# Attention and a spectral filter interleaved on one core: a constant table loaded later, softmax normalization with due times, and a newly searched order

## The chip, the core and the metric

The kernel runs on one core of one Trainium2 chip. The metric is device time in microseconds of one execution. A core has five engines with a queue of instructions each: TensorE (PE) for matrix products, VectorE (DVE), ScalarE (ACT), GpSimd (POOL) and SyncE (SP), which here only issues DMA transfers. An instruction waits on semaphores that other engines or transfers raise, and every queue is worked off strictly in order.

## The reference

Two independent computations are put side by side in the output, 2048 rows of 448 + 448 columns.

```python
# A: attention, S = 2048, D = 448, 16 heads of 28
q, k, v = split(A_x @ A_wqkv)
p = softmax(q @ k^T * 28 ** -0.5)
a = (p @ v) @ A_wo
# B: a filter in the frequency domain, S = 2048, D = 448
X = rfft2(B_x) * (B_w_r + 1j * B_w_i)
b = irfft2(X, s=(2048, 448))
out = concatenate([a, b], axis=-1)
```

## The kernel before, in words

**Attention.** The heads are taken in 4 groups of 4 and the queries in 4 chunks of 512, which gives 16 blocks. In a block, keys come in 16 chunks of 128. A unit is one head, one key chunk and 512 queries: its scores fill one of the 7 working PSUM banks (L1083). For most units ACT computes the exponential, two or three banks in one instruction (L1109), into a ring of 14 SBUF buffers. For a few key chunks in each block (`DN`, L304, usually 3 of 16) DVE does it instead: one instruction turns scores into integers whose bits read as a bf16 power of two (L1119), three more make shifted copies of a pair of units (L1127), and four products with scaled copies of V average the error away. DVE's units have 8 buffers. The products of both kinds accumulate in the eighth bank, `ACC` (L1178), where a column of ones in V gives the softmax sums; a block's products are all made before the next block's begin.

**End of a block.** `finish` (L1202) copies `ACC` to a buffer `oaug` (DVE, L1281), queues a small PE job `n1` that gathers the sums, takes their reciprocal on DVE (L1246), queues a PE job `n2` that spreads them over the partitions (L1255), and multiplies on DVE (L1275). Both jobs are queued with due time -2, ahead of everything else; there are 2 buffers `oaug`. When the last group is done, products with `wo` give the output rows, which are copied and stored.

**Filter.** The transforms along the rows are products with constant tables. Since the transform is symmetric, row n of `B_x` is first added to and subtracted from row 1024 - n (`fold_all`, L653, on POOL). For this, two SyncE transfers (L1409) write rows in reverse order to a DRAM buffer `xrev`: first rows 1 to 255 and then 256 to 511, of two planes each. From there L1413 reads 127 rows and L1414 reads 128 rows of each plane into the tile R1a, and L1416 the rest. Folding writes R1b. Then come products with the 1 MB table FR (`load_f`, L594), a product with T1, the multiplication with the filter W on POOL, and the same back with table T2. W is reversed in DRAM too (`rev_w`, L609).

**How the order is made.** The program that builds the kernel simulates the engines with estimated costs and writes each queue as it goes. `defer` (L149) puts DVE and POOL work in a list with a due time, and `flush` (L186) commits an entry when its inputs are ready by the estimate. `later` (L183) holds a DMA back until its input is ready by the estimate. `dma` estimates a landing as the transfers queued so far, at `kb`/280 us each, plus 2 us plus a `lag`. PE jobs, such as projections or transforms, have due times counted in units that ACT has been given (`st["ai"]`); `JIT` shifts the due times of single jobs, and `PH` places the phases of the filter. [...] Constants set the rest: `FMAX` is the most units of one fill, `TH1` the backlog of ACT from which a single unit may go, `DLEAD` how many units DVE's share may run ahead, and `AL_C` the slack of L1127. A filler product keeps PE active where it would be idle.

Transfers wait for all earlier transfers on their semaphore that were issued when the waiting instruction was written: the first fold with a reversed row therefore waits for both L1413 and L1414 of a plane.

The lines around the moved transfer, in the order in which SyncE gets them:

```python
            for hf in range(2):
                P.dma("sp", ... xrev ..., "d_rv%d" % hf, writes=[("xrev", hf)], kb=2500)
                # held until xrev is ready: L1413, L1414, then L1416 with after=late_loads
        for i in range(2):
            P.dma("sp", ... xE ..., "d_xe", writes=[("xE", i)], kb=2)
        P.dma("sp", ... alt ..., "d_t", writes=["alt"], kb=130)
        load_f(0, 0)
```

## Time and profile before

| | |
|---|---|
| median of 4 runs | 424.44 us (423.23 to 426.2) |
| the profiled execution | 423.46 us, of it 421.7 us span |
| ACT exponentials L1109 | 366 instructions, 384.1 us busy, 828 units |
| of these by shape | 250 of two banks, 106 of three, 10 of one |
| DVE L1119 and L1127 | 196 and 294 instructions, 132.8 and 109.8 us |
| POOL | 190 instructions, 153.3 us |
| first and last exponential | starts at 11.86 us, ends at 413.84 us |
| mean TensorE clock granted | 0.988 |

The profile is one execution. Its busy time is the union of an engine's instructions. The slices cut the span into 40 equal parts of 10.5 us, and a digit is the busy share in tenths. In the list of waits a row reads: engine and line that waited, what released it, total, times, longest, in microseconds. In the order of time a row reads: start, duration, engine, line, operation, tiles written and read, count; in brackets stands how long the engine was idle before and what released it.

### The profile page before, as it was taken

How to read it: one execution, taken by the hardware profiler on the slowest of the kernel's cores; microseconds unless marked ns; L12 is line 12 of the kernel's file. 1: busy time of each engine (PE TensorE's matmuls, PEld its weight loads, DVE VectorE, ACT ScalarE, POOL GpSimd, SP SyncE). 2: the span in 40 equal slices, each digit the busy share in tenths (PEclk: the TensorE clock that was granted, in tenths of full speed). 3: DMA queues.
4: the chain of work that ended last, by engine and by line, in shares of the span. 5: the costliest groups of instructions: out<-in, count | busy, mean ns of one | idle time of the engine just before them, and what ended most of it. 6: DMA issues, size and time to landing. Idle time of an engine off the chain costs nothing.

```text
span 421.7 us, 15264 instructions
## 1 busy us (share of the span) xinstructions
PE 388.1 (92%) x6610; PEld 140.1 (33%) x6611; DVE 341.8 (81%) x717; ACT 388.7 (92%) x374; POOL 153.3 (36%) x190
## 2 busy tenths in 40 slices
PE   8999648999999999899989999999999999989995
PEld 4443212323433333233332333322334333333332
DVE  4789549969697998899869897887898889879972
ACT  2899739999999999999999999999999999999994
POOL 6422054574702554665653455308335100000000
PEclk9999959999999999999999999999999999999999
DMA  9814245200011003400000000000000011101111
GB/s 192 211 49 146 86 143 126 51 4 2 4 38 31 2 3 118 96 3 2 3 2 2 4 2 2 4 2 2 2 3 3 23 35 46 56 24 56 36 45 46
DMA packets 25079, 17.96 MB, mean 43 GB/s; under 512 B 14642, under 2 KB 24372, under 8 KB 24628
## 3 DMA queue, kind: packets, MB, share of 16 engines
q1 hardware_dynamic: 23620, 16.49, 14.0%
q8 instruction: 52, 0.85, 0.8%
q10 hardware_dynamic: 1392, 0.50, 0.5%
q14 instruction: 15, 0.12, 0.1%
HBM read 11.73 MB, written 5.39 MB: 41 GB/s over the span
## 4 chain that ended last, share of the span: by engine, by line
PE 44%; ACT 18%; DVE 13%; SPq 10%; POOL 6%; issue 5%; DMA 2%; ACTq 0%; DVEq 0%; POOLq 0%
ACT ET L1109 17%; PE PS L527 16%; PE PS L1083 14%; PE PS L1178 13%; DVE TT L1127 5%; DVE TT L1119 4%; POOL R1b L664 3%; SPq L1419 2%; DMA R1a<-xrev 2%; SPq L1409 2%; POOL ptmp L664 2%; SPq L1414 2%; SPq L455 2%; POOL R L651 1%; PE PS L1646 1%
## 5 line engine op out<-in xcount | busy, mean ns | idle before, releaser
L1109 ACT ACTIVATE ET<-PS 128x1024 bf16<-128x1024 f32 (+2 forms) x366 | 384.1, 1161 | 19.5 <-PE PS L1083 18.0
L1083 PE MATMUL PS<-qT,kT 28*128 28x512 bf16 x1024 | 141.9, 386 | 21.4 <-DVE TT L1119 9.9
L1119 DVE TENSOR_SCALAR TT<-PS 128x512 int16<-128x512 f32 x196 | 132.8, 685 | 22.9 <-PE PS L1083 21.3
L1127 DVE TENSOR_SCALAR TT<-TT 128x1024 int16<-128x1024 int16 x294 | 109.8, 420 | 17.8 <-POOL R1b L664 12.4
L1178 PE MATMUL PS<-ET,Vaug 128*32 128x512 bf16 x828 | 81.8, 389 | 2.5 <-ACT ET L1109 1.0
L1083 PEld LDWEIGHTS PS<-qT,kT 28*128 28x128 bf16 x1024 | 35.5, 91 | 137.2 <-ACT ET L1109 81.5
L651 POOL TENSOR_TENSOR ptmp<-R1a,R1b 128x450 f32<-128x450 bf16 x32 | 31.4, 995 | 37.9 <-DVE TT L1127 21.4
L1178 PE MATMUL PS<-TT,Vs 128*32 128x512 bf16 x588 | 40.8, 384 | 0.0
L582 POOL TENSOR_SCALAR Vs<-Vaug 128x128 bf16<-128x128 bf16 x42 | 22.2, 530 | 45.3 <-DVE TT L1127 40.8
L527 PE MATMUL PS<-T,R 112*32 112x450 bf16 (+2 forms) x512 | 35.1, 357 | 0.3 <-DVE TT L1119 0.2
L1178 PEld LDWEIGHTS PS<-ET,Vaug 128*32 128x32 bf16 x828 | 21.1, 93 | 42.0 <-issue 31.0
L651 POOL TENSOR_TENSOR R<-R1b 113x512 bf16<-113x512 f32 (+3 forms) x16 | 20.1, 1277 | 27.5 <-DVE TT L1127 17.2
L664 POOL TENSOR_TENSOR ptmp<-R1a 128x448 f32<-128x448 bf16 x16 | 16.4, 1034 | 23.4 <-DMA R1a<-xrev 12.6
L651 POOL TENSOR_TENSOR R1a<-ptmp 128x225 bf16<-128x225 f32 x32 | 18.0, 582 | 18.9 <-DVE TT L1127 16.6
L664 POOL TENSOR_TENSOR R1b<-ptmp 128x448 bf16<-128x448 f32 (+1 forms) x17 | 19.0, 1127 | 6.7 <-DVE TT L1127 6.3
L1178 PEld LDWEIGHTS PS<-TT,Vs 128*32 128x32 bf16 x588 | 15.8, 98 | 14.2 <-DVE TT L1127 0.5
L527 PE MATMUL PS<-FR,R1b 128*32 128x512 bf16 (+1 forms) x256 | 19.7, 382 | 0.6 <-POOL R1b L664 0.5
L651 POOL TENSOR_TENSOR ptmp<-ptmp 128x450 f32<-128x450 f32 x16 | 15.6, 983 | 12.1 <-DVE TT L1127 12.1
L527 PE MATMUL PS<-wv,xAT 128*32 128x112 bf16 x1024 | 19.8, 214 | 0.1
L527 PE MATMUL PS<-FR,R1a 128*32 128x512 bf16 (+2 forms) x256 | 19.7, 383 | 0.1
L1178 PE MATMUL PS<-TT,Vaug 128*32 128x512 bf16 x196 | 19.5, 387 | 0.1
L527 PE MATMUL PS<-xAT,wq 128*32 128x512 bf16 x240 | 18.9, 383 | 0.2 <-DVE TT L1119 0.2
(92 smaller groups left out, 309.4 us busy)
## 6 DMA issues: line engine op xcount, KB each, us to landing
out_dram<-wst SPq DMA_DIRECT2D x30, 112.0 KB, 1.7
FR<-cst_tab SPq DMA_DIRECT2D x3, 1024.0 KB, 7.5
R1a<-in_B_x_dram SPq DMA_DIRECT2D x2, 448.0 KB, 4.5
R1b<-wrev SPq DMA_DIRECT2D x14, 56.2 KB, 2.4
wst<-in_A_wqkv_dram SPq DMA_DIRECT2D x2, 252.0 KB, 3.1
T<-cst_t SPq DMA_DIRECT2D x1, 450.0 KB, 8.2
R1b<-in_B_w_r_dram SPq DMA_DIRECT2D x8, 56.2 KB, 2.2
R1b<-in_B_w_i_dram SPq DMA_DIRECT2D x8, 56.2 KB, 2.1
```

The lines of the kernel that those rows point to most:

```text
L455: P.dma("sp", lambda e: e.dma_start_transpose(xAT[:, 0:3, 512 * n:512 * n + 512], src[:, 0:384]), "d_x%d" % n, writes=[("xAT", n, 0)], kb=700)
L527: ins = e.matmul(out[c:c1], lhsT[:, c:c1], rhs, start=start, stop=stop, tile_position=(0, c))
L582: P.defer("pool", lambda e, ki=ki, kc=kc, c=c: e.tensor_scalar(Vs[:, g % 2, ki, c - 1, :], Vaug[:, g % 2, kc, :], WS[c], None, ALU.mult), ...
L651: P.defer(eng, lambda e: e.tensor_tensor(out, a, b, op), reads=reads, writes=writes, busy=c, allow=allow, port=True, after=after)
L664: P.defer("pool", lambda e: e.tensor_tensor(out, a, b, o), reads=reads, writes=writes, busy=cost, allow=al, port=True, after=after)
L1083: ins = e.matmul(bank(bk), kT[32 * j:32 * j + DH, g % 2, 128 * kc:128 * (kc + 1)], qT[32 * j:32 * j + DH, b % QSL, :], start=True, stop=Tr ...
L1109: P.op("act", lambda e: e.activation(dst, src, ACT.Exp, scale=ESC), reads=[("B", i) for i in o], writes=[("E", p + k) for k in range(n)], ...
L1119: P.defer("dve", lambda e, bk=bk, slot=slot: e.tensor_scalar(TT[:, 0, slot, :], bank(bk), BIAS, 0.0, ALU.add, ALU.max), reads=[("B", bk)], ...
L1127: P.defer("dve", lambda e, c=c, slot=slot: e.tensor_scalar(TT[:, c, slot - 1:slot + 1, :], TT[:, 0, slot - 1:slot + 1, :], SHF * c, None, ...
L1178: ins = e.matmul(ACC[32 * j:32 * j + 32, :], lh, rhs, start=first, stop=last, tile_position=(0, 32 * j))
L1409: P.dma("sp", lambda e, n0=n0, n1=n1: e.dma_start(xrev[:, n0:n1, :], B_x[0].rearrange("(a p) d -> a p d", a=2)[:, 1024 - n0:1024 - n1:-1, :]),
L1414: P.later("sp", lambda e, a=a: e.dma_start(xB[:, a, 1, :], xrev[a - 2, 128:256]), "d_xb%d" % a, [("xrev", 0)], [("xB", a, 1)], 112, lag=1.0)
```

## The change

- `load_f(0, 0)`, the load of the first FR table, moves from its place ahead of the held row transfers into `late_loads`, which runs after the last of them; the other loads in `late_loads` were there already.
- The estimate of the reversal rises from `kb` 2500 to 2650, and the held row transfers are all given a lag of `XLAG` = 3.0 (before: none or 1.0).
- `n1` and `n2` are due 8 and 10 or 18 units later, except in the last group, with 4 buffers instead of 2. (`rb` and `zr`, which this path doesn't use, are not allocated. A form that normalizes two blocks at once is added but off: `PAIR` is `False`.)
- In block 11 DVE takes 3 key chunks instead of 4.
- Output rows of the filter may be copied by ACT once all exponentials have been issued. `YT`, which would move the last such jobs behind the attention, is 0.
- `DLEAD`, `FMAX`, `TH1`, `AL_C` and four entries of `JIT` are new.

```diff
-DN = (3, 3, 3, 3, 3, 3, 3, 3, 3, 3, 2, 4, 3, 3, 4, 3)
+DN = (3, 3, 3, 3, 3, 3, 3, 3, 3, 3, 2, 3, 3, 3, 4, 3)
...
-DBL, NDF, DLEAD = 2.5917, 1, 16
+DBL, NDF, DLEAD = 2.5917, 1, 8
...
-FMAX, FMIN, TH1, RMAX, KEEP, KMIN = 3, 2, 0.4784, 1, 2, 3
+FMAX, FMIN, TH1, RMAX, KEEP, KMIN = 4, 2, 0.5154, 1, 2, 3
...
+JIT gets 122: -9.6, 68: -13.8, 135: 7.0, 93: 19.3
...
-FAL, NAL, NLAG = 6.0, 8.0, 3.0
+YT, PAIR = 0, False
+FAL, NAL, NLAG, XLAG = 6.0, 8.0, 3.0, 3.0
...
-AL_D, AL_C, AL_E = 0.7783, 3.6896, 0.9444
+AL_D, AL_C, AL_E = 0.7783, 5.0, 0.9444
...
-        NO = 4 if NDMA else 2
+        NO = 4
...
# y_job, end:
+                if st["ai"] >= NA and not P.blocked((mk,), (("astg", slot),)) and P.free["act"] < P.free["dve"] + 0.3:
+                    P.op("act", lambda e: e.activation(astg[:, slot, :], M[:, 0:448], ACT.Copy), reads=[mk], writes=[("astg", slot)], busy=0.43)
+                    after()
+                else:
+                    evac(lambda e: e.tensor_copy(astg[:, slot, :], M[:, 0:448]), mk, [("astg", slot)], 448, G["AL_E"], after=after)
...
# finish:
-                        after=lambda: add(("n2", g, qc), -2, [("rz", i), "cid"], mms2, end2, n=128))
+                    add_n2((g, qc, i, mms2, end2))
...
-                    after=lambda: add(("n1", g, qc), -2, [("oaug", i), "cid"], mms1, end1, n=64))
+                    add(("n1", g, qc), st["ai"] + 8 if g < NG - 1 else -2, [("oaug", ii) for ii in n1i] + ["cid"], mms1, end1, n=64)
...
+        def add_n2(x):
+            g, qc, i, mms2, end2 = x
+            late = g < NG - 1
+            add(("n2", g, qc), (st["ai"] + 10 + 8 * (qc % 2)) if late else -2, [("rz", i), "cid"], mms2, end2, n=128)
...
         def late_loads():
             if PFOLD:
                 fold_all()
+            load_f(0, 0)
             load_f(1, 1)
...
-                      "d_rv%d" % hf, writes=[("xrev", hf)], kb=2500)
+                      "d_rv%d" % hf, writes=[("xrev", hf)], kb=2650)
...
-        load_f(0, 0)
```

In the same lines the held transfers L1413, L1414 and L1416 get `lag=XLAG`.

## The prediction

> **What bounds the kernel now.** I read the busy rows first, then the slices, then the waits, and then the order of time where the slices show a hole.

> ```profile
> PE 388.1 (92%) x6610; PEld 140.1 (33%) x6611; DVE 341.8 (81%) x717; ACT 388.7 (92%) x374; POOL 153.3 (36%) x190
> ...
> PE   8999648999999999899989999999999999989995
> DVE  4789549969697998899869897887898889879972
> ACT  2899739999999999999999999999999999999994
> PEclk9999959999999999999999999999999999999999
> ```

> ACT has 388.7 us of work in 421.7 and is full in nearly every slice; PE's row holds filler matmuls too. The exception is slices 4 and 5 (42 to 63 us), where ACT, PE and DVE empty together and the PE clock falls. The waits name the chain:

> ```profile
> POOL ptmp L664 <- DMA R1a<-xrev: 12.6, 1, 12.6
> ...
> DVE TT L1127 <- POOL R1b L664: 12.4, 6, 9.4
> ...
> PE PS L1083 <- DVE TT L1119: 9.9, 4, 9.2
> ...
> ACT ET L1109 <- PE PS L1083: 18.0, 24, 9.0
> ```

> One single wait of POOL for reversed rows is passed on from engine to engine. Why the rows are late stands in SyncE's issues, and how long DVE stands still in its own order of time:

> ```profile
> 26.69 10.45 SPq L1419 DMA_DIRECT2D ptmp<-in_B_x_dram  x2
> 37.19 0.36 SPq L1422 DMA_DIRECT2D alt<-cst_alt  x1
> 37.59 0.43 SPq L596 DMA_DIRECT2D FR<-cst_tab  x1
> 38.14 0.24 SPq L1413 DMA_DIRECT2D R1a<-xrev  x1
> 38.42 6.49 SPq L1414 DMA_DIRECT2D R1a<-xrev  x1
> 44.96 0.31 SPq L1413 DMA_DIRECT2D R1a<-xrev  x1
> 45.31 4.59 SPq L1414 DMA_DIRECT2D R1a<-xrev  x1
> ```

> ```profile
> 47.43 0.68 DVE L1119 TENSOR_SCALAR TT<-PS 128x512 int16<-128x512 f32 x1
> 57.52 0.43 DVE L1127 TENSOR_SCALAR TT<-TT 128x1024 int16<-128x1024 int16 x1 [9.41 <-POOL R1b L664]
> ```

> ```profile
> 55.18 1.03 POOL L664 TENSOR_TENSOR ptmp<-R1a 128x448 f32<-128x448 bf16 x1 [12.63 <-DMA R1a<-xrev]
> ```

> The 1 MB table (L596) stands right ahead of the four row transfers. The critical chain has the rows landing at 55.05 (45.31 + 9.74). POOL then does two operations and DVE goes on at 57.52, which is 2.47 after landing. DVE stood for 9.41, ACT for 8.96 (from 50.44). Outside this hole ACT is nearly saturated: from 200 to 280 it is busy 79.97 of 80 us. After the hole, in the low clock, it loses another 0.28 + 0.65 = 0.93. Its remaining small gaps between the first exponential at 11.86 and the last at 413.84 make about 7 us.

> [...] while the two-plane reversal runs, the DMA share is 0.14 (2 of 16 is 0.125), and from 46 to 50 us it is 0.10, near one engine. [...] (clock 0.50 from 56 to 63 us, PE idle 9.21 before).

> **The change, part by part.**

> Table 0 behind the rows (`load_f(0, 0)`). In the packet records the table is 128 packets of 8 KB, 8 for each engine, about 331 ns each: 2.65 us on the one engine[...]. On that engine the reversal ends about 41.5, the table about 44.5, then come 127 rows at 38 ns = 4.8 us, 8 rows of the next transfer, 127 again, 8 again: 54.7, plus completion, which is the 55.05. Without the table everything from 44.5 moves up by 2.65: landing at 52.4. The two blocked issues (6.49, 4.59)[...] add no second gain; I bound the further gain by 0 and 1 us and take 0. The table itself is then issued after the last rows, with the other table, about 49 us. Its first user is the matmul FR,R1b at 86.9, so that delay is hidden by some 28 us. What is queued behind it (table 1, the reversal of W, T1, T2, the output weights) loses the 2.65 that it gained; POOL and ACT queues are not passed.

> Due times of the rows (`kb` 2650, `XLAG`). These move no transfer; they decide where in DVE's and POOL's queues the folds stand. The kernel's own bookkeeping up to `alt` gives 38.87. Before: + 3.66 (table) + 3 x 0.4 (rows) + 2 = 45.73 for the first fold that needs reversed rows. After: + 1.07 (twice 150/280) + 1.2 + 2 + 3 (lag) = 46.14. This clock agreed with the trace: fold and follow-up would end about 48, and DVE ran dry at 48.11. So the folds are queued only 0.4 later, while rows land at 52.4. DVE meets the wait between 48.5 and, if one more group of L1127 (one each 2.1 us) goes first, 50.6; it goes on at 52.4 + 2.47 = 54.9. Stall 4.3 to 6.4 instead of 9.41; ACT gains 3.1 to 5.1, I take **-4.0**. The low clock still comes (PE idle near 5 us), so its 0.93 stays. If the new order were to put the folds well later, the whole 8.96 + 0.93 goes; if earlier, the gain shrinks to 2.2.

> One unit less for DVE in block 11 (`DN` 4 to 3). 196 L1119 become 192 and 294 L1127 become 288: DVE saves 4 x 0.685 + 6 x 0.420 = 5.3 us, PE 12 groups of products. ACT gets four banks more, 828 to 832. By shape an exponential takes 1049 ns for two banks and 1476 for three, so a bank costs 427 ns; the mean sum of 424.7 against 384.1 busy gives 0.111 overlap each, so one instruction more costs 1049 - 854 - 111 = 84 ns. 4 x 0.427 + 1.8 x 0.084 = **+1.86**, on the path. Against it: from 298 to 326, around block 11, ACT is busy 26.08 of 28 and PE 27.23, its worst stretch after the hole. The freed DVE and PE should give back part of the 1.9: I take **-1.0**, bounds 0 and -1.9.

> Normalizing products with a due time, four buffers. The counts stay (16 reciprocals of 0.25, L1255 0.40 a block). What the urgent form costs is small: the waits on the reciprocal that reach PE are 0.9 + 0.2 (L1083) and 0.9 + 0.3 (L1255), none reaches ACT. The queues behind the waiting reciprocal are DVE's; it now comes when its product is made. A buffer is reused four blocks later, some 100 us, against a delay of 10 to 18 banks, some 9 us at 0.47 us a bank: no wait. The last group, whose result the end needs, keeps its urgency. Taken with the search (four new offsets, `DLEAD` 8, `AL_C` 5.0, `FMAX` 4, `TH1`): **-0.5**, bounds -3 (about half of ACT's small gaps) and +3 (some 36 exponentials more at 84 ns). A four-bank fill is two two-bank exponentials, and with one backlog on ACT six free banks are rare, so I expect their number to stay near 366.

> Output evacuation on ACT after the last exponential: the 16 L905 are done by 395.6 now, before the last exponential at 413.84, so nothing happens; nor with `PAIR` and `YT` off. The tail of 7.9 us stays.

> Sum: -4.0 + 1.86 - 1.0 - 0.5 = -3.6. The profiled execution took 423.46 (span 421.7 and 1.8 around it): 419.8. The median of four runs is 424.44, 0.98 above it, so for the median **420.8**.

> **The rivals.** (1) The hole closes: the new order puts the folds behind 4 to 6 us of other DVE work. For it: folds have no user before 86.9, so there is room. Against it: the due time rose by 0.4 only. Then -8.96 - 0.93 + 1.86 - 1.0 - 0.5 = -9.5: 414.9. (2) The change doesn't do what it says: the hole shrinks by the 2.2 that remain if folds are met early, and the four banks eat it, with nothing from block 11 and the search: -2.2 + 1.86 = -0.3: 424.1. (3) Slower: late products. DVE's units may lead by 8 instead of 16 and their shifted copies are due later (5.0 for 3.69), while each block's products must finish before the next block's begin and only 14 exponential buffers, some 6.6 us of ACT, bridge it. If every one of 16 block ends then costs ACT 0.5 us, +8 - 3.6 = +4.4: 428.8. It is level at 0.23 us a block and slower by over 0.5% from 0.36. Against it: eight unit buffers already limit the lead, and DVE gets 5.3 us of room. For it: ACT's 0.03 us idle from 200 to 280 can only get worse.

> **How the numbers follow.** Forecast 0.50, hole closed 0.20, nothing moved 0.13, late products 0.17. 0.5% is 2.1 us, about what a measurement of this kernel tells from no change: faster means under 422.3, slower over 426.6. The forecast's own range is 418 to 423.5, so 0.45 of its 0.50 is faster and 0.05 the same; with the closed hole faster is 0.65, the same 0.17 (0.05 + 0.12), slower 0.18 (0.17 + 0.01). The range runs from 413.5, the closed hole with a little from the search, to 426; it leaves out most of the late products and a tip at the low end.

> **What would show it.** The FR issue behind both L1416 issues; reversed rows landing near 52.4; L1127's longest wait for POOL 4 to 6.5 instead of 9.4 and ACT's longest for PE 4 to 6; 832 banks in 360 to 385 exponentials; less ACT idle around 300 to 325; no waits at block ends. I am wrong if the rows land as late as before, if DVE meets them without a wait, or if ACT has new gaps beyond 70 us that add up to over 3 us.

## The result, and the profile after

| | before | changed |
|---|---|---|
| median | 424.94 us (56 runs) | 424.94 us (35 runs) |
| ratio, 95% interval | | 0.9994 (0.9978 to 1.001) |
| profiled execution, its span | 423.46, 421.7 us | 422.96, 421.1 us |
| mean TensorE clock in it | 0.988 | 0.984 |

No change that can be measured, where 0.9% less had been forecast. The hole did shrink. Lines are numbered a little higher in the changed kernel: its L1114, L1088, L1124, L1132, L665, L1440 and L1441 are L1109, L1083, L1119, L1127, L664, L1413 and L1414 of the kernel before. First the busy times and slices of the changed kernel:

```profile
PE 392.3 (93%) x6662; PEld 141.0 (33%) x6663; DVE 337.7 (80%) x707; ACT 390.2 (93%) x373; POOL 151.9 (36%) x187
...
ACT  2899937999999999989999999999999999999994
...
PEclk9999958999999999999999999999999999999999
```

ACT's loss has moved from slices 4 and 5 (7, then 3) to slices 5 and 6 (3, then 7) and is no smaller there, and the clock is low in two slices (5, then 8) instead of one. The waits (engine, what released it, total, times, longest):

```profile
ACT ET L1114 <- PE PS L1088: 16.0, 23, 5.0
...
POOL ptmp L665 <- DMA R1a<-xrev: 8.1, 1, 8.1
...
DVE TT L1132 <- POOL R1b L665: 6.6, 3, 5.8
...
PE PS L1088 <- DVE Vaug L589: 5.3, 1, 5.3
```

The chain is the one of before. The program has L1132 wait on a semaphore for the last POOL operation committed before it, also when that operation makes nothing that L1132 reads, and POOL's operations on the last L1132. PE's wait ends with a DVE copy (`Vaug`) that stood in the queue behind DVE's own wait. SyncE, DVE and POOL around the hole, each in order of time:

```profile
37.53 0.22 SPq L1440 DMA_DIRECT2D R1a<-xrev  x1
37.79 4.44 SPq L1441 DMA_DIRECT2D R1a<-xrev  x1
42.27 0.31 SPq L1440 DMA_DIRECT2D R1a<-xrev  x1
42.63 4.58 SPq L1441 DMA_DIRECT2D R1a<-xrev  x1
...
48.24 0.95 SPq L597 DMA_DIRECT2D FR<-cst_tab  x2
```

```profile
48.19 0.68 DVE L560 CAST qT<-PS 128x512 bf16<-128x512 f32 x1
54.66 0.76 DVE L1132 TENSOR_SCALAR TT<-TT 128x1024 int16<-128x1024 int16 x2 [5.80 <-POOL R1b L665]
```

```profile
52.40 1.03 POOL L665 TENSOR_TENSOR ptmp<-R1a 128x448 f32<-128x448 bf16 x1 [8.14 <-DMA R1a<-xrev]
```

The table is issued after the rows. These land at 52.27 by the critical chain (forecast 52.4), POOL starts on them at 52.40, DVE stands for 5.80 (4.3 to 6.4) and ACT for 5.00, 3.96 less than before (4.0). What comes after the hole is new. ACT in order of time, before:

```profile
59.40 1.02 ACT L1109 ACTIVATE ET<-PS 128x1024 bf16<-128x1024 f32 x1 [8.96 <-PE PS L1083]
60.71 2.36 ACT L1109 ACTIVATE ET<-PS 128x1536 bf16<-128x1536 f32 x2 [0.28 <-PE PS L1083]
63.72 3.71 ACT L1109 ACTIVATE ET<-PS 128x1536 bf16<-128x1536 f32 x3 [0.65 <-PE PS L1083]
```

After:

```profile
57.32 1.02 ACT L1114 ACTIVATE ET<-PS 128x1024 bf16<-128x1024 f32 x1 [5.00 <-PE PS L1088]
58.62 1.02 ACT L1114 ACTIVATE ET<-PS 128x1024 bf16<-128x1024 f32 x1 [0.27 <-PE PS L1088]
60.13 1.02 ACT L1114 ACTIVATE ET<-PS 128x1024 bf16<-128x1024 f32 x1 [0.49 <-PE PS L1088]
61.59 1.02 ACT L1114 ACTIVATE ET<-PS 128x1024 bf16<-128x1024 f32 x1 [0.43 <-PE PS L1088]
64.88 1.45 ACT L1114 ACTIVATE ET<-PS 128x1536 bf16<-128x1536 f32 x1 [2.27 <-PE PS L1088]
66.76 4.20 ACT L1114 ACTIVATE ET<-PS 128x1024 bf16<-128x1024 f32 x4 [0.42 <-PE PS L1088]
```

After the hole ACT waits again for PE's scores before each of the next five exponentials, 3.9 us in all. What PE does meanwhile stands in the stretches of one microsecond. Columns: stretch, length, busy time (instructions) of PE, PEld, DVE, ACT, POOL, then clock, DMA share and GB/s. Before:

```profile
62.00:63.00 1.00, 1.00 (x16) 0.16 (x6) 0.06 (x1) 1.00 (x2) 0.77 (x2) 0.50 0.23 48
63.00:64.00 1.00, 1.00 (x20) 0.33 (x16) 0.34 (x1) 0.35 (x2) 0.30 (x1) 0.95 0.25 52
```

After:

```profile
63.00:64.00 1.00, 1.00 (x12) 0.16 (x4) 0.00 (x0) 0.00 (x0) 1.00 (x2) 0.50 0.26 43
...
65.00:66.00 1.00, 1.00 (x16) 0.32 (x8) 0.52 (x1) 1.00 (x1) 0.59 (x1) 0.54 0.31 68
66.00:67.00 1.00, 1.00 (x19) 0.29 (x11) 0.30 (x1) 0.57 (x2) 0.00 (x0) 1.00 0.31 63
```

PE is busy throughout, at half clock, until 65.9 us; before, the clock was back at 63.1. The clock records have it low for 10.24 us before (52.9 to 63.1, of which PE worked 4.4) and for 13.65 after (52.3 to 65.9, of which PE worked 9.3). PE came back 2.1 us earlier (56.61 for 58.69) and got its clock back 2.8 us later.

The account, from every exponential's start and end in the records (in us; "gaps low" are those in or within 1 us after a low clock, the hole apart; "tail" is from the last exponential to the end of the span):

| kernel | first starts | busy | hole | gaps low | other gaps | last ends | tail |
|---|---|---|---|---|---|---|---|
| before | 11.86 | 384.1 | 8.96 | 0.93 | 8.01 | 413.84 | 7.81 |
| changed | 11.71 | 385.5 | 5.00 | 3.89 | 7.63 | 413.77 | 7.36 |
| difference | -0.15 | +1.4 | -3.96 | +2.96 | -0.38 | | -0.45 |

The differences add up to -0.6, the difference of the spans.

This is an account of one execution of each kernel. Of the others, the mean granted clock is on record, but not where it was low. Over all of them the low clock is no longer than before: the mean is 0.981 in the changed kernel (36 executions) and 0.981 in the kernel before (135, on the chips of the experiments). Where the mean is 0.987 or 0.988, so 10 to 11 us of low clock, the changed kernel has a median of 422.8 us (8 executions) and the kernel before 423.4 (30; chips differ by up to 0.8). Even with equally long low clock, only some 0.6 of the forecast 3.6 us is there, so a longer low clock alone doesn't explain the loss. The PE work that falls into it (9.3 us for 4.4 in the two profiles) could explain it, and the first experiment tests that.

### The profile page after: what moved, and what is told of

It reads as the page before. It is cut to its first block, busy times and chain, and to the rows that moved or that the text cites. A ratio compares the mean times of both kernels' runs of the same rounds, so it can differ in the third digit from the quotient of the medians.

```text
span 421.1 us, 15342 instructions
## 1 busy us (share of the span) xinstructions
PE 392.3 (93%) x6662; PEld 141.0 (33%) x6663; DVE 337.7 (80%) x707; ACT 390.2 (93%) x373; POOL 151.9 (36%) x187
## 4 chain that ended last, share of the span: by engine, by line
PE 51%; ACT 18%; DVE 11%; SPq 10%; issue 5%; POOL 3%; DMA 2%; DVEq 0%; ACTq 0%; POOLq 0%
PE PS L528 19%; ACT ET L1114 18%; PE PS L1088 16%; PE PS L1183 15%; DVE TT L1132 4%; SPq L1446 2%; DVE TT L1124 2%; DMA R1a<-xrev 2%; SPq L1436 2%; POOL R1b L665 2%; SPq L456 2%; SPq L1441 1%; PE PS L1674 1%; POOL ptmp L665 1%; SPq L457 1%
## 5 line engine op out<-in xcount | busy, mean ns | idle before, releaser
L1114 ACT ACTIVATE ET<-PS 128x1024 bf16<-128x1024 f32 (+2 forms) x365 | 385.5, 1175 | 18.1 <-PE PS L1088 16.0
L1088 PE MATMUL PS<-qT,kT 28*128 28x512 bf16 x1024 | 141.7, 387 | 15.4 <-ACT ET L1114 6.8
L1124 DVE TENSOR_SCALAR TT<-PS 128x512 int16<-128x512 f32 x192 | 130.7, 685 | 26.6 <-PE PS L1088 25.0
L1132 DVE TENSOR_SCALAR TT<-TT 128x1024 int16<-128x1024 int16 x288 | 108.8, 419 | 14.8 <-POOL R1b L665 6.6
L1088 PEld LDWEIGHTS PS<-qT,kT 28*128 28x128 bf16 x1024 | 35.0, 91 | 131.4 <-ACT ET L1114 74.3
L583 POOL TENSOR_SCALAR Vs<-Vaug 128x128 bf16<-128x128 bf16 x39 | 20.6, 530 | 39.0 <-DVE TT L1132 37.4
L665 POOL TENSOR_TENSOR ptmp<-R1a 128x448 f32<-128x448 bf16 x16 | 16.4, 1033 | 23.7 <-DVE TT L1132 15.2
L665 POOL TENSOR_TENSOR R1b<-ptmp 128x448 bf16<-128x448 f32 (+1 forms) x17 | 19.0, 1130 | 13.0 <-DVE TT L1132 12.8
```

The lines of the kernel that those rows point to most:

```text
L583: P.defer("pool", lambda e, ki=ki, kc=kc, c=c: e.tensor_scalar(Vs[:, g % 2, ki, c - 1, :], Vaug[:, g % 2, kc, :], WS[c], None, ALU.mult), ...
L665: P.defer("pool", lambda e: e.tensor_tensor(out, a, b, o), reads=reads, writes=writes, busy=cost, allow=al, port=True, after=after)
L1088: ins = e.matmul(bank(bk), kT[32 * j:32 * j + DH, g % 2, 128 * kc:128 * (kc + 1)], qT[32 * j:32 * j + DH, b % QSL, :], start=True, stop=Tr ...
L1114: P.op("act", lambda e: e.activation(dst, src, ACT.Exp, scale=ESC), reads=[("B", i) for i in o], writes=[("E", p + k) for k in range(n)], ...
L1124: P.defer("dve", lambda e, bk=bk, slot=slot: e.tensor_scalar(TT[:, 0, slot, :], bank(bk), BIAS, 0.0, ALU.add, ALU.max), reads=[("B", bk)], ...
L1132: P.defer("dve", lambda e, c=c, slot=slot: e.tensor_scalar(TT[:, c, slot - 1:slot + 1, :], TT[:, 0, slot - 1:slot + 1, :], SHF * c, None, ...
```

## The experiments

The theory after the result: the hole shrank as worked out, and the low clock after it and ACT's four banks took the gain back. The rival: the new order loses it on its own, with its two-bank fills and its waits between DVE and POOL. All ratios are to the kernel before on the same chip.

**Clock kept, hole kept.**

```diff
# in fill(), ahead of the score products that PE stands in front of (ai == 85, the units given to ACT so far; in the kernel before: 82, 40 times)
+            if st["ai"] == 85 and n and "hole" not in st:
+                st["hole"] = True
+                fb = [0]
+                t_ = P.free["pe"]
...
+                for _ in range(22):
+                    P.op("pe", keep, reads=["cid"], writes=[("B", fb[0])], busy=0.0)
+                P.free["pe"] = t_
```

> The changed kernel with 22 filler products (256 columns in two halves, 4.7 us at full clock) put into PE's queue at the place where PE stands still for 5.35 us; nothing else is moved. They compute nothing that is used. Clock theory: the hole itself stays at 5.0 us on ACT, the clock does not fall, and ACT's gaps after the hole fall from 3.9 to under 1, so 3 us less, near 422, ratio 0.993. Rival: the gaps after the hole come from the order and stay; no change, 425.

> The kernel before with 40 such filler products (8.6 us) where its PE stands still for 9.21 us. Clock theory: only the 0.93 us that ACT lost in its low clock can come back, near 424, ratio 0.998. Rival: no change.

The changed kernel: 422.43 us, ratio 0.9949 (0.9929 to 0.9969). The kernel before: 424.89 us, 1.0012 (0.9992 to 1.0032). ACT of the changed kernel with fillers, in order of time:

```profile
46.08 7.60 ACT L1128 ACTIVATE ET<-PS 128x1024 bf16<-128x1024 f32 x8 [0.22 <-PE PS L1088]
60.18 3.77 ACT L1128 ACTIVATE ET<-PS 128x1024 bf16<-128x1024 f32 x4 [6.50 <-PE PS L1088]
64.42 6.46 ACT L1128 ACTIVATE ET<-PS 128x1536 bf16<-128x1536 f32 x6 [0.47 <-PE PS L1088]
```

The clock doesn't fall in this execution: every slice of its clock row is 9, the mean 1.0. Gaps of 3.9 us have become 0.47 with the same exponentials in the same order. The hole is 1.5 us longer, because the fillers keep PE until 59.76: its scores follow 4.5 us after DVE goes on (59.69 after 55.21), and 1.95 us after in the changed kernel. The median is 2.5 us lower (1.9 by the two ratios, as the chips differ), where the clock theory expected 3 and the rival, for which these gaps belong to the order, none; the rival falls. In the kernel before there was only 0.93 to win: too little to see, and its profile has a low clock again (8 in the clock row from 317 to 328 us, mean 0.996).

Both filler runs are on one chip. Their executions in which the clock hardly fell (mean 0.999 or 1.0) have medians of 421.4 us for the changed kernel (4 executions) and 423.9 for the kernel before (6). They are 2.5 us apart, and the holes in the two profiles 2.1 (6.50 and 8.60). Without the low clock, the shorter hole is worth what it measures.

**Rows faster, queues the same.**

```diff
-P.later("sp", lambda e, a=a: e.dma_start(xB[1:128, a, 0, :], xrev[a - 2, 1:128]), ...
+P.later("sp", [lambda e, a=a, p0=p0, p1=p1: e.dma_start(xB[p0:p1, a, 0, :], xrev[a - 2, p0:p1]) for p0, p1 in ((1, 113), (113, 128))], ...
```

> The changed kernel, with each transfer of 127 reversed rows split into one of 112 and one of 15[...]; the order of the other queues is as in the changed kernel. The clock theory (the hole shrank by 4 us as worked out, and the low clock that follows it grew from 10.2 to 13.7 us and cost ACT 3 us more): rows land near 43 us, DVE meets them without a wait, no hole, no low clock after the start, ACT gains 5.0 + 3.9, so near 416 us, ratio 0.979. The rival (the new order loses the rest on its own, in two-bank fills and in waits between DVE and POOL, whatever the clock): only the 5.0 of the hole goes, near 420 us.

> The kernel before with the same split of the 127-row transfers; the queues of PE, DVE, ACT and POOL are the same as before, instruction by instruction. Clock theory: the hole of 8.96 us and the 0.93 after it go, near 415 us, ratio 0.977. With the changed kernel split at 417.9, that would mean that the rest of the change (one more ACT chunk, due times, new order) costs some 3 us once the hole is out of the way. Rival (the new order is the better one and only the hole's clock hid it): above 418.

Changed kernel, split: 417.94 us, 0.9836 (0.9795 to 0.9877). Kernel before, split: **415.74 us, 0.9797 (0.9754 to 0.9841)**, better than both kernels by 9.2 us. Each is measured by 6 executions. The first lies halfway between the two theories (416 and 420) and doesn't separate them; the second is where the clock theory put it. The DVE and POOL of the kernel before, split, at the place of the old hole:

```profile
48.24 0.68 DVE L1119 TENSOR_SCALAR TT<-PS 128x512 int16<-128x512 f32 x1
49.33 0.43 DVE L1127 TENSOR_SCALAR TT<-TT 128x1024 int16<-128x1024 int16 x1 [0.41 <-POOL R1b L664]
```

```profile
46.97 1.04 POOL L664 TENSOR_TENSOR ptmp<-R1a 128x448 f32<-128x448 bf16 x1 [3.61 <-DMA R1a<-xrev]
```

The same two DVE instructions that lay 9.41 us apart now have 0.41 between them, with the table still ahead of the rows. POOL starts on the rows 8 us earlier (46.97 for 55.18), and SyncE's two L1414 issues take 0.38 us each instead of 6.49 and 4.59. In the packet records of the kernel before, 79 rows of 896 bytes move from 47 to 50 us, 41 ns each and one begun every 38 ns: one row at a time, 23 to 24 GB/s from 47 to 49 us. The records don't name the engines; that one of 16 moves these rows, as the forecast took, is an estimate from this. In the account, split against split, the changed kernel has busy +1.0 (385.4 for 384.4), gaps low +1.1, the first exponential +0.5, other gaps +0.1, tail -0.4. Both executions still have low clocks late, which the expectation had not: the clock row has an 8 from 135 to 146 and from 302 to 312 us in the changed kernel, and from 311 to 321 in the one before. So without the hole the rest of the change is worth nothing or a little less; the two intervals overlap, so how much less isn't settled.

**Folds queued later, rows as they are.**

```diff
-FAL, NAL, NLAG, XLAG = 6.0, 8.0, 3.0, 3.0
+FAL, NAL, NLAG, XLAG = 6.0, 8.0, 3.0, 9.0
```

> The changed kernel with the estimated lag of the row transfers at 9 instead of 3 us: nothing moves on the DMA queues, but the folds are written into DVE's and POOL's queues 6 us later, after the rows' real landing at 52.3. Clock theory: no hole, no low clock, near 416 us, as with the split rows. Rival: near 420. If the hole were due to something else than the queued position of the folds, it would stay, near 425.

427.44 us, 1.0058 (1.0034 to 1.0082). The hole at 50 us is gone, and POOL starts on the reversed rows at 55.55 without a wait: so the folds' place in the queues makes the hole. But there is another one, seen in ACT's order of time:

```profile
150.59 2.65 ACT L1114 ACTIVATE ET<-PS 128x1536 bf16<-128x1536 f32 x3 [5.13 <-PE PS L1088]
```

Just before, from 145 to 151 us, PE is busy with transforms (FR,R1b), projections of the next group and products with T. Why they meet there isn't shown. It isn't that the transforms begin later: the first FR,R1b product runs at 80.48 us, and at 85.82 in the changed kernel. Both theories, which expected 416 and 420, missed this, and of the clock the run says nothing. All of ACT's gaps together are 18.3 us, for 16.5 in the changed kernel: closing the hole in this way moved the order behind it.

**The table's place, alone and undone.**

```diff
# kernel before, table moved
+            load_f(0, 0)
             load_f(1, 1)
...
-        load_f(0, 0)
# changed kernel, table back: the reverse
```

> The kernel before with the table's load moved behind the rows and nothing else, the estimates left as they were. Rows land 2.65 us earlier, near 52.4, but the estimate for them falls by 3.66 us, so the folds are queued that much earlier too, and DVE runs dry near 45: the hole is 9 to 10.5 us, as long as before. Near 424 to 427. If landing alone counted, the hole would be 6.3 us and the time near 422.

> The changed kernel with the table's load back ahead of the rows. Rows land at 55 again; the estimate rises by 3.66 us, so the folds are queued later by as much: hole on DVE 4.5 to 6 us, about as in the changed kernel, and the time within 1 us of it (424 to 426) but for where the clock's windows fall and what the shifted order does. If landing alone counted: hole 8.5 us, 428.

Moved alone: 431.49 us, 1.0167 (1.0133 to 1.0201). Put back: 428.18 us, 1.0079 (1.0051 to 1.0108). The waits of the kernel before with the table moved:

```profile
DVE TT L1127 <- POOL ptmp L664: 11.1, 5, 8.6
...
POOL ptmp L664 <- DMA R1a<-xrev: 9.8, 1, 9.8
```

and of the changed kernel with the table back:

```profile
POOL ptmp L665 <- DMA R1a<-xrev: 11.4, 1, 11.4
...
DVE TT L1132 <- POOL ptmp L665: 5.7, 2, 5.3
```

Four kernels now cross the two edits. ACT's hole is 8.96 us with neither, 8.08 with the table moved alone, 5.23 with the estimates raised alone (the changed kernel with the table back) and 5.00 with both. Moving the table brings the rows 2.6 to 2.9 us earlier (POOL starts on them at 52.57 for 55.18, and at 52.40 for 55.27), yet shortens the hole by 0.9 and 0.2 only, because the folds are queued earlier by about as much. The raised estimates shorten it by 3.7 and 3.1. So the hole shrank because the folds were queued later, not because the rows landed earlier; the rest of the change is in both kernels with raised estimates, and its share isn't separated. DVE's own hole was expected at 9 to 10.5 us with the table moved alone and at 4.5 to 6 with it back, and was 8.56 and 5.27. The expected times, 424 to 427 and 424 to 426, were missed. Both kernels are worse than that explains, by 6 and 3 us: their later gaps grew (in the account, low and other together 17.1 and 14.9 for 8.9 and 11.5), since the whole order behind is another one.

**Single parts on kernels without the hole.** Five edits: urgent due times, four chunks or the old constants again, in the changed kernel with split rows; the new due times or three chunks, in the kernel before with split rows.

```diff
# as_norm_urgent (bs_norm_due: the reverse, with NO = 4)
-                    add(("n1", g, qc), st["ai"] + 8 if g < NG - 1 else -2, ...
+                    add(("n1", g, qc), -2, ...
-            add(("n2", g, qc), (st["ai"] + 10 + 8 * (qc % 2)) if late else -2, ...
+            add(("n2", g, qc), -2, ...
# as_dn4 (bs_dn3: the reverse)
-DN = (3, 3, 3, 3, 3, 3, 3, 3, 3, 3, 2, 3, 3, 3, 4, 3)
+DN = (3, 3, 3, 3, 3, 3, 3, 3, 3, 3, 2, 4, 3, 3, 4, 3)
# as_old_order: DLEAD 16, FMAX 3, TH1 0.4784, AL_C 3.6896, four entries of JIT out
```

> The changed kernel with split rows, and the normalizing products urgent again (due -2 in every group; four buffers kept). By the forecast the due times are worth 0 to 1 us: 418 to 419 against the 417.9 of the split alone. If the due times are what the new order lives from, 420 or more; if they cost, under 417.

> The kernel before with split rows and the normalizing products' due times and four buffers; nothing else. By the forecast 0 to 1 us less: 414.7 to 415.7. If a part without its own search disturbs the order: 418 or more, as the reverse edit did in the changed kernel (417.9 to 425.8).

> The changed kernel with split rows and four key chunks for DVE in block 11 again. ACT saves 1.9 us of work; by the forecast the net is +0.9 for the three chunks, so 417. If the disturbed order costs more than the work saves: 419 or more.

> The kernel before with split rows (415.7) and three key chunks instead of four for DVE in block 11; nothing else. ACT's own time rises by 1.9 us. By the forecast 1.0 of it comes back around block 11: 416.6, and at best 415.7. If every part disturbs an order that was searched without it, it costs more than its work: 418 or more, with gaps spread behind the point where the queues first differ.

> The changed kernel with split rows, and the constants of the order as before (lead 16, three banks at most, threshold 0.4784, slack 3.69, the four new offsets of job times out). By the forecast the search is worth 0.5 us, from -3 to +3: 415 to 421. If due times, three chunks and offsets only work together: 421 or more.

| edit | base | median us | ratio to before, interval |
|---|---|---|---|
| due times urgent | 417.94 | 425.78 | 1.0022 (0.9999 to 1.0045) |
| due times added | 415.74 | 423.17 | 0.9938 (0.9913 to 0.9962) |
| four chunks | 417.94 | 422.14 | 0.9930 (0.9907 to 0.9953) |
| three chunks | 415.74 | 421.17 | 0.9914 (0.9884 to 0.9944) |
| old constants | 417.94 | 423.81 | 0.9968 (0.9947 to 0.9990) |

Every one costs 4 to 8 us, in whichever direction it is made: adding the due times costs 7.4 (6.0 by the ratios) and taking them away 7.8. ACT's work explains 0.1 to 2.2 of it (busy 385.2 to 387.6); the rest are gaps everywhere, such as 14.0 us of other gaps for 8.6 with the due times added. No price of a part can be read from such runs. What they suggest is that a searched order is worth 4 to 8 us against a neighbour that wasn't searched, more than any part of this change; that the search is the reason wasn't tried, for instance by searching anew after one of the edits.

## Why the prediction was wrong

- **The bound and the chain** were right: split rows take the hole and 9.2 us away with all other queues unchanged.
- **Table 0 behind the rows:** landing 52.4 forecast, 52.27 measured; SyncE's blocked issues 4.44 and 4.58, no second gain, as taken. Hidden delay of the table: no wait for it, as said.
- **Due times of the rows:** DVE's stall 5.80, ACT's gain 3.96 for the -4.0 taken. Right, as a sum of the move and the estimates. Taken apart, it is the estimates' gain: without the move they leave 5.23 of the hole, with it 5.00.
- **The step that failed** is in the same part: "The low clock still comes (PE idle near 5 us), so its 0.93 stays." It was 3.89 in the profiled execution. The low clock was taken as a fixed cost of any hole. What it cost went with the PE work that fell into it: 4.4 us of such work before, 9.3 after, because PE came back earlier (56.61 for 58.69) and the clock later (65.92 for 63.10). The filler run (gaps 0.47, 2.5 us faster) shows that these gaps are the clock's. The size 2.96 is of this pair of executions.
- **One unit less in block 11:** ACT's busy time rose 1.4 for the +1.86, since exponentials of three banks became more (117 for 106) and the number 365. A gain around block 11 was there as well, though that the third chunk alone made it isn't shown. The stretches of the changed kernel:

```profile
298.00:326.00 28.00, 27.21 (x602) 10.67 (x602) 23.52 (x49) 27.47 (x26) 11.80 (x14) 1.00 0.01 3
```

  ACT is busy 27.47 of 28 for 26.08 before, 1.4 more (forecast 1.0).
- **Due times and search, -0.5:** other gaps fell by 0.38 in all. With the 1.4 won around block 11, gaps elsewhere grew by about 1.0; start and tail gave 0.6 back. Within the bounds of -3 to +3.
- **The rivals:** late products at block ends didn't come: other gaps are 7.63 for 8.01. The hole that closes was had by splitting the rows, not by the order, and closing it in the queues alone (lag 9) cost more than it brought. The rival "doesn't do what it says" (424.1) has about the right time, but by other terms: it took the hole's gain as 2.2 and kept the low clock at 0.93.
- **Two readings:** ACT's small gaps before were 8.0 us, not "about 7", which moves only the bound of -3. A DMA share of 0.10 from 46 to 50 us is 1.6 of 16 engines and not "near one"; from 47 to 49 us the share is 0.07, 1.1 of 16, and the packet records show one row at a time.
- **The signs:** the rows' landing, the longest waits (5.80 and 5.00), 832 banks in 365 exponentials and the fuller block 11 all came as named. None of the signs concerned the ten microseconds after the hole.

Forecast -3.6, measured -0.6 in the profiled span: +2.96 is the clock, the rest are small terms that cancel. That the two medians come out equal is an accident of such terms.

## What to carry to other kernels

When a hole is shortened, price what follows it by the PE work that falls into the low clock (9.3 us here for 4.4 before), not by what followed the old hole; filler products in a known PE wait kept the clock (mean 1.0 in the profile; about 2 us here, nothing in the kernel before). Look first at how fast the late transfer itself moves (one row at a time here, 23 to 24 GB/s): one line that splits 127 rows into 112 and 15 was worth 9 us, the reordering of transfers and queues nothing. Moving a transfer helps little where a planner moves the waiting work along with it. In this searched schedule, each of the eight edits that moved the queues behind it made the kernel 2.5 to 8 us slower, so test causes with edits that leave the queues as they are.

## What the runs showed of the hardware

| kernel | stretch, us | clock in it, and after it | PE busy, us | columns |
|---|---|---|---|---|
| before | 49.45 to 52.86 | 1.00, 0.50 | 0.03 | 0 |
| before | 52.86 to 56.27 | 0.50, 0.50 | 0.00 | 0 |
| before | 56.27 to 59.69 | 0.50, 0.50 | 1.00 | 4608 |
| before | 59.69 to 63.10 | 0.50, 1.00 | 3.41 | 12800 |
| changed | 48.86 to 52.27 | 1.00, 0.50 | 2.13 | 10880 |
| changed | 52.27 to 55.68 | 0.50, 0.50 | 0.00 | 0 |
| changed | 55.68 to 59.10 | 0.50, 0.50 | 2.49 | 9216 |
| changed | 59.10 to 62.51 | 0.50, 0.50 | 3.41 | 12288 |
| changed | 62.51 to 65.92 | 0.50, 1.00 | 3.41 | 14336 |

All other stretches between 20 and 417 us had 11462 columns or more and were followed by full clock. In the half clock, PE's busy time doesn't tell the stretch after which the clock came back from the one after which it didn't: 3.41 us each, in the changed kernel from 59.10 and from 62.51. The columns do tell them apart in these two executions (12800 and 14336 for at most 12288), but two profiles don't show that the columns decide it. Two scores of one fill (L1088 x2) and four (x4) both took 0.61 us at half clock, so fills of two banks brought half as many columns in the same time; that this made the difference between 12288 and 12800 wasn't tried.

The clock also fell without a hole, in the executions with split rows: the mean granted clock is 0.991 in the changed kernel and 0.996 in the one before, which makes about 7.5 and 3.3 us of half clock, an estimate from these means and the spans of 416.6 and 414.2 us. In the kernel before with split rows the clock was 0.91 from 298 to 318 us, while PE was busy 18.99 of the 20 us.
